# Softmax and key-stage transposes moved to VectorE blocks, values loaded in long runs, in a fused attention and two-layer kernel

## The chip, the cores and the metric

One core of a Trainium2 chip runs the whole program. The metric is the device time of one execution in microseconds (us): the median of the runs, all of them on the chip. The engines have separate in-order queues: TensorE (PE, with its weight loads PEld), VectorE (DVE), ScalarE (ACT), GpSimd (POOL), and SyncE (SP), which in this kernel only issues DMAs.

## The reference

```python
def sm_attn(qq, kk, vv):
    s = scale * np.matmul(qq, kk.transpose(0, 1, 3, 2))
    s = s - np.max(s, axis=-1, keepdims=True)
    a = np.exp(s)
    a = a / (np.sum(a, axis=-1, keepdims=True) + 1e-09)
    return np.matmul(a, vv)
p_packed = sm_attn(p, k, v)          # 32 packed rows attend over 576 keys
out = sm_attn(q, p_packed, p_packed) # 576 queries attend over the 32
...
xn = x / rms * rms_g                 # x: (4608, 512), RMS norm over 512
g = xn @ w_gate
silu = g * (1.0 / (1.0 + np.exp(-g)))
val = xn @ w_val
x = silu * val @ w_out
...
h = x @ w_in
g = h * np.cos(h)
return (g @ w_out).astype(np.float32)
```

Sizes: batch 8, 8 heads, 576 positions, head width 64, 32 packed rows; 4608 tokens of 512; inner widths 1536 and 2048. The arrays q, k, v, p are float32; the weights of the first layer and of the second come as 64-bit floats and are narrowed on the chip.

## The kernel before

The program has four stretches, and a hand-written order (`manual_schedule`) fixes the sequence on every engine in the first three.

**Key stage.** A loop `for i in range(NG + 2)` runs over 16 units (8 batches, two groups of 4 heads). SP loads the packed rows (`load_k`: `pn`, and the keys `kn`, 128 rows with runs of 4608 bytes) four units ahead and the values (`load_v`) two units ahead. The values go in three DMAs of 192 KB, each to 32 partitions in runs of 1536 bytes, into a tile `vn` with 16 rows of padding. For a unit, PE transposes the keys (`u_kt`, tile `kp`, copied by ACT into `kT`), multiplies packed rows with keys (`u_s1`, tile `s1`; for units below `S_PAD` = 11 by a weight tile padded to 128 columns), DVE takes the maximum, ACT the exponential (`u_e`, tile `e`). `u_et` of the unit before transposes the exponentials: six PE transposes into `et`, two ACT copies into `eT`. `u_pp` multiplies them with the values: 6 chunks of 96 positions times 4 heads, each a product of 128 rows by 32 columns by 64; a float32 product is two passes on PE, so 48 passes. `u_fin` transposes the result and stores it to DRAM. Between these, weights of the first layer are narrowed on DVE (`narrow_b`, `wy`, `ny`), and three `unit` calls multiply packed values with weights (`mps`).

**Query attention.** `attend(b)` is a generator. Each `next` on it emits one step. Steps: transposes of queries (`qtp`, copied by ACT to `qT`), scores `sp` (32 packed rows by 288 queries for 4 heads, in two PSUM banks), a copy to `sT` (one half on ACT, one on DVE), PE transposes `stp`, maximum and subtraction on DVE from PSUM into `s` (96 rows), two exponentials on ACT, sums, reciprocals and products on DVE, PE transposes `atp` back with ACT copies into `at`, then products `xp` whose squares give the RMS factor (`a_x`), the root (`a_r`, a POOL power), its spread over rows (`a_b`, transposes `rb`, DVE products) and a split in two parts (`a_p`). `ATT_ORD` and `ATT_ORD0` give the order of the last part, and "-" is an empty step. `attend(0)` runs in the key stage from unit 5 on: one step in iteration 5 and three in each later one, `ATT_U` = 31 in all.

**First layer.** For each batch, 24 iterations: `gv_block` (12 products of 128 by 128 by 288), a silu, a product, a split, and `acc_block` (6 products of 128 by 128 by 512) for the iteration three back. `att_step` spreads the 37 steps of `attend(b + 1)` over the 48 half iterations of batch b, so seven attentions run here, for batches 1 to 7. All of this shares the four PSUM buffers `mm`.

**Second layer.** `h_block` and `o_block`, over 9 chunks of 512 tokens and 16 tiles of 128.

SP's queue issues all DMAs in program order.

Of the kernel before, what the change touches and what calls it, by code (L numbers as in the profile page):

```python
# [20 lines left out]
def kernel(  # L21
# [20 lines left out]
    CP = 96  # L42
# [19 lines left out]
    REST = S - 512  # L62
    V_P = 16
# [154 lines left out]
    def attend(b):  # L218
        s = a1.tile([CP, NC_, H, NP], F32, tag="s", name="s")
        for g in range(2):  # L220
            qTs = []
            for j in (2 * g, 2 * g + 1):
                qv = qn.pop(4 * b + j)
                qT = a2.tile([128, 2, HALF], F32, tag="qT", name="qT")
                for i in range(2):
                    tp = psb[0].tile([128, HALF], F32, tag="mm", name="qtp")
                    for c in range(CH):
                        nc.tensor.transpose(  # L228
                            tp[:, c * CP:(c + 1) * CP], qv[:, i, 2 * c:2 * c + 2, :].rearrange("p c d -> p (c d)"),
                            ident[:CP, :CP],  # L230
                        )
                    nc.scalar.activation(out=qT[:, i], in_=tp, func=AF.Copy)
# [12 lines left out]
            nc.scalar.activation(out=sT[:, 0], in_=sp[0], func=AF.Copy)  # L245
            nc.vector.tensor_copy(sT[:, 1], sp[1])
            yield
            for r in range(2):
                st_p = psb[0].tile([CP, CH, 4, NP], F32, tag="mm", name="stp")
                for c in range(CH):  # L250
                    nc.tensor.transpose(
                        st_p[:, c].rearrange("p h n -> p (h n)"), sT[:, r, c * CP:(c + 1) * CP], ident
                    )
                mx = a2.tile([CP, CH, 4], F32, tag="amx", name="amx")
                nc.vector.tensor_reduce(out=mx, in_=st_p, op=ALU.max, axis=AX.X)
                nc.vector.tensor_tensor(
                    out=s.rearrange("p (c t) h n -> p c t h n", t=2)[:, :, r, 4 * g:4 * g + 4, :], in0=st_p,
                    in1=mx.unsqueeze(3).to_broadcast([CP, CH, 4, NP]), op=ALU.subtract,
                )
            yield  # L260
        n_s = 8 * CH
        hv = [s[:, hf * CH:(hf + 1) * CH].rearrange("p c h n -> p (c h) n") for hf in range(2)]
        for sf in hv:
            nc.scalar.activation(out=sf, in_=sf, func=AF.Exp, scale=scale)
            yield "e"
        for sf in hv:
            sm = a2.tile([CP, 2, n_s], F32, tag="sm", name="sm")
# [4 lines left out]
            if b:  # L272
                yield
            nc.vector.tensor_tensor(
                out=sf, in0=sf, in1=sm[:, 1].unsqueeze(2).to_broadcast([CP, n_s, NP]), op=ALU.mult
            )
            yield

        def transposed(hf, kt):
            tp = psb[0].tile([128, HALF], F32, tag="mm", name="atp")  # L280
            for c in range(CH):
                nc.tensor.transpose(
                    tp[:, c * CP:(c + 1) * CP],
                    s[:, hf * CH + c, 4 * kt:4 * kt + 4, :].rearrange("p h n -> p (h n)"), ident[:CP, :CP],
                )
            return tp

        z = {}

        def a_t(hf, kt):  # L290
            if (hf, kt) == (0, 0):
# [33 lines left out]

        def a_b(hf, _):
            at, ri = z["at"], z["ri"]
            rb = psb[0].tile([128, HALF], F32, tag="mm", name="rb")
            for c in range(CH):
                nc.tensor.transpose(  # L330
                    rb[:, c * CP:(c + 1) * CP], ri[:, 1, 2 * c + hf:2 * c + hf + 1].to_broadcast([CP, 128]),
                    ident[:CP, :CP],
                )
            nc.vector.tensor_tensor(
                out=at[:, :, hf], in0=at[:, :, hf], in1=rb.unsqueeze(1).to_broadcast([128, 2, HALF]), op=ALU.mult
            )

# [10 lines left out]

    v_t = [u2.tile([128, 4, NC_, D], F32, tag=f"vn{x}", name="vn", bufs=1) for x in range(3)]
    for x in range(2):  # L350
        nc.vector.memset(v_t[x], 0.0)
    e_pad = u2.tile([128, 2 * V_P + S], F32, tag="e", name="e", bufs=1)
    for x in (slice(0, V_P), slice(V_P + S, 2 * V_P + S)):
        nc.vector.memset(e_pad[:, x], 0.0)
    nat_k, nat_v = {}, {}
# [39 lines left out]
    def u_kt(i, ms):  # L395

        z = st[i]
        kT, kn = z["kT"], z["kn"]
        kv = kT.rearrange("q h (t m p) -> q h t m p", t=CH, m=CH)
        for m in ms:  # L400
            kp = ps_2.tile([128, CH * 128], F32, tag="kp", name="kp")
            for t in range(CH):
                r = 2 * (CH * m + t)
                nc.tensor.transpose(
                    kp[:, t * 128:(t + 1) * 128], kn[:, r:r + 2, :].rearrange("p c d -> p (c d)"), ident
                )
            nc.scalar.activation(
                out=kv[:, :, :, m, :], in_=kp.rearrange("q (t h p) -> q h t p", t=CH, h=4), func=AF.Copy
            )
# [21 lines left out]
    def u_e(i):  # L431
        z = st[i]
        s1, mx = z["s1"], z["mx"]
        e = e_pad[:, V_P:V_P + S].rearrange("p (a s) -> p a s", a=2)
        nc.scalar.activation(
# [3 lines left out]
    def u_et(i):  # L439
        z = st[i]  # L440
        eT = u2.tile([128, NC_, 128], F32, tag="eT", name="eT", bufs=1)
        for hf in range(2):
            et = ps_2.tile([128, CH, 128], F32, tag="kp", name="et")
            for c in range(CH):
# [7 lines left out]
    def u_pp(i):  # L452
# [179 lines left out]
    u_kt(0, range(CH))  # L632
    nc.gpsimd.memset(v_t[2], 0.0)
    w_q, wo_q = [], []
# [370 lines left out]
    def o_out(n, t):  # L1005
# [8 lines left out]
        while off < 128:  # L1014
            if n < B:
                b, u = n, t * 128 + off
            else:
                b, u = divmod(t * 128 + off, REST)
                u += TOK
            c, pp = divmod(u, CP)  # L1020
            m = min(128 - off, CP - pp)
            dst = out[b * S:(b + 1) * S].rearrange("(p c) d -> c p d", c=NC_)[c, pp:pp + m, :]
# [58 lines left out]
```

## Time and profile before

| quantity | value |
|---|---|
| runs | 1687.13, 1689.0, 1690.26 us; median 1689.0 |
| span of the profiled execution | 1681.2 us |
| between that span and the median | 7.8 us |
| PE busy | 1628.8 us, 97% of the span |
| DVE, ACT, POOL busy | 60%, 50%, 4% |
| key stage | 0 to about 155 us |
| first layer | about 155 to 860 us |
| second layer | about 860 us to the end |

The profile is of one execution. Its span runs from the first to the last instruction; the device time of a run also holds what lies before and after. No device time of the profiled execution itself is listed, so the span stands for it, and the 7.8 us are taken as constant. PE's busy time overstates its work, since matmuls overlap and their ends are modelled: the cost of a group is read from the starts of what comes before and after it.

### The profile page before, as it was taken

The numbers are of one execution on the slowest core, as the hardware profiler recorded it, in microseconds if no ns is written. First come the engines' busy times: TensorE is split into PE (matmuls) and PEld (weight loads), VectorE is DVE, ScalarE is ACT, GpSimd is POOL, SyncE is SP. The second block draws the span as 40 slices with busy tenths as digits, with TensorE's granted clock in tenths as the row PEclk, the third lists the DMA queues.
The fourth block names the chain that finished last, engine by engine and source line by source line (L and its number), as shares of the span: only waits on it lengthen the run. The fifth ranks groups of instructions, "written<-read, shape, count | busy, mean of one in ns | idle before, by whom it ended". The sixth has DMA issues, their size and how long they took to land.

```text
span 1681.2 us, 26128 instructions
## 1 busy us (share of the span) xinstructions
PE 1628.8 (97%) x10112; PEld 1325.8 (79%) x10112; DVE 1008.5 (60%) x1890; ACT 845.2 (50%) x1587; POOL 73.9 (4%) x74
## 2 busy tenths in 40 slices
PE   7877999999999999999999999999999999999998
PEld 5545868788888788888888888888888888888887
DVE  3577985566565666665435665656565656565554
ACT  4455555455454545454434554545454545454443
POOL 1001430000000000000110000000000000000000
PEclk9887999999999999999999999999999999999999
DMA  9996744454535454544363020101010101000001
GB/s 253 285 247 173 226 158 153 145 183 139 195 120 179 143 176 144 170 127 131 104 239 106 25 63 1 51 1 51 0 50 1 50 1 41 11 0 26 1 26 25
DMA packets 103580, 177.35 MB, mean 105 GB/s; under 512 B 39456, under 2 KB 55840, under 8 KB 103456
## 3 DMA queue, kind: packets, MB, share of 16 engines
q1 hardware_dynamic: 103456, 175.68, 34.4%
q8 instruction: 80, 1.31, 0.3%
q14 instruction: 44, 0.36, 0.1%
HBM read 134.22 MB, written 41.42 MB: 104 GB/s over the span
## 4 chain that ended last, share of the span: by engine, by line
PE 89%; DMA 5%; DVE 3%; ACT 1%; issue 1%; SPq 1%; POOL 0%; DVEq 0%; POOLq 0%; ACTq 0%
PE hp L160 8%; PE hp L159 8%; PE hp L158 8%; PE ops L160 8%; PE ops L159 8%; PE ops L158 8%; PE gv L158 6%; PE acc L158 6%; PE gv L159 6%; PE gv L160 6%; PE acc L160 6%; PE acc L159 6%; PE mps L580 3%; DMA kn<-in_k_dram 2%; PE qtp L228 1%
## 5 line engine op out<-in xcount | busy, mean ns | idle before, releaser
L158 PE MATMUL gv<-apt,wmhl 128*128 128x288 f32 x768 | 237.8, 310 | 3.0 <-DVE silu L766 2.0
L159 PE MATMUL gv<-apt,wmhl 128*128 128x288 f32 x768 | 228.6, 298 | 0.2 <-DVE apt L107 0.2
L160 PE MATMUL gv<-apt,wmhl 128*128 128x288 f32 x768 | 228.0, 297 | 0.0
L159 PE MATMUL hp<-xhl,wmhl 128*128 128x512 f32 x576 | 224.1, 389 | 0.0
L160 PE MATMUL hp<-xhl,wmhl 128*128 128x512 f32 x576 | 224.1, 389 | 0.0
L158 PE MATMUL ops<-w2hl,ghl 128*128 128x512 f32 x576 | 224.1, 389 | 0.0
L159 PE MATMUL ops<-w2hl,ghl 128*128 128x512 f32 x576 | 224.1, 389 | 0.0
L158 PE MATMUL hp<-xhl,wmhl 128*128 128x512 f32 x576 | 223.9, 389 | 0.0
L160 PE MATMUL ops<-w2hl,ghl 128*128 128x512 f32 x576 | 222.3, 389 | 0.0
L981 ACT ACTIVATE r<-r 128x512 f32<-128x512 f32 x144 | 91.1, 633 | 250.0 <-DVE r L980 250.0
L989 DVE TENSOR_TENSOR r<-r,hp 128x512 f32<-128x512 f32 x144 | 98.9, 687 | 164.8 <-ACT r L982 164.8
L158 PEld LDWEIGHTS gv<-apt,wmhl 128*128 128x128 f32 x768 | 146.0, 190 | 44.3 <-issue 17.6
L158 PE MATMUL acc<-shl,wohl 128*128 128x512 f32 x432 | 176.6, 409 | 0.2 <-DMA shl<-s 0.2
L160 PE MATMUL acc<-shl,wohl 128*128 128x512 f32 x432 | 170.7, 395 | 2.4 <-POOL wohl L546 2.4
L159 PE MATMUL acc<-shl,wohl 128*128 128x512 f32 x432 | 169.6, 393 | 0.0
L773 ACT ACTIVATE shl<-silu 128x288 fp32r<-128x288 f32 x192 | 85.4, 445 | 159.6 <-DVE silu L766 158.4
L766 DVE TENSOR_TENSOR silu<-silu,gv 128x288 f32<-128x288 f32 x192 | 86.5, 451 | 125.5 <-PE gv L160 106.2
L976 ACT ACTIVATE kk<-hp,magic 128x512 f32<-128x512 f32 x144 | 99.1, 688 | 117.3 <-PE hp L160 117.1
L159 PEld LDWEIGHTS gv<-apt,wmhl 128*128 128x128 f32 x768 | 146.2, 190 | 4.4 <-DVE apt L107 0.5
L160 PEld LDWEIGHTS gv<-apt,wmhl 128*128 128x128 f32 x768 | 145.8, 190 | 0.0
L977 DVE TENSOR_SCALAR kk<-kk 128x512 f32<-128x512 f32 x144 | 61.4, 426 | 116.1 <-ACT kk L976 116.0
L158 PEld LDWEIGHTS ops<-w2hl,ghl 128*128 128x128 f32 x576 | 108.2, 188 | 22.6
(127 smaller groups left out, 2708.4 us busy)
## 6 DMA issues: line engine op xcount, KB each, us to landing
wy<-wy SPq DMA_DIRECT2D x96, 512.0 KB, 4.5
kn<-in_k_dram SPq DMA_DIRECT2D x16, 576.0 KB, 7.4
vn<-in_v_dram SPq DMA_DIRECT2D x48, 192.0 KB, 6.5
qnat<-in_q_dram SPq DMA_DIRECT2D x32, 288.0 KB, 4.1
x_dram<-x SPq DMA_DIRECT2D x18, 512.0 KB, 3.0
x1raw<-x_dram SPq DMA_DIRECT2D x18, 512.0 KB, 4.0
raw<-in_moe_w_in_dram SPq DMA_DIRECT2D x16, 512.0 KB, 4.2
raw<-in_moe_w_out_dram SPq DMA_DIRECT2D x16, 512.0 KB, 4.2
```

What stands on the lines that cost most here:

```text
L158: nc.tensor.matmul(ps, lhi, rhi, start=first, stop=False)
L159: nc.tensor.matmul(ps, lhi, rlo, start=False, stop=False)
L160: nc.tensor.matmul(ps, llo, rhi, start=False, stop=last)
L228: nc.tensor.transpose(tp[:, c * CP:(c + 1) * CP], qv[:, i, 2 * c:2 * c + 2, :].rearrange("p c d -> p (c d)"), ident[:CP, :CP],)
L580: nc.tensor.matmul(ps[kt][h * NP:(h + 1) * NP], ppT[b // 4][rows, 4 * kt + h, n:n + NP], w_y[2 * u + kt][rows, j], start=True, stop=True,)
L766: nc.vector.tensor_tensor(out=t, in0=t, in1=pss[1], op=ALU.mult)
L773: nc.scalar.activation(out=sh[:, 0, cols], in_=t, func=AF.Copy)
L976: nc.scalar.activation(out=kk, in_=hp, func=AF.Identity, scale=1.0 / TWO_PI, bias=magic[:, 0:1])
L977: nc.vector.tensor_scalar(out=kk, in0=kk, scalar1=-MAGIC, scalar2=None, op0=ALU.add)
L981: nc.scalar.activation(out=r, in_=r, func=AF.Abs)
L989: nc.vector.tensor_tensor(out=r, in0=r, in1=hp, op=ALU.mult)
```

## The change

- Scores `sp` are transposed by DVE, in blocks of 32 by 32, straight from PSUM into a tile `st` of 128 rows; `sT`, `stp` and their copies go. Maximum and subtraction run on 128 rows by 576, and so do sums and products. The exponential is one ACT instruction over 128 rows by 1152.
- The weights go back by one DVE block transpose per group of heads (`a_t`), without PE and ACT.
- In the key stage one DVE block transpose of 128 by 576 replaces six PE transposes and two ACT copies (`u_et`). The values are loaded by one DMA per unit, 128 rows with runs of 4608 bytes, and three memsets go. `u_pp` runs 18 chunks of 32 positions times 4 heads, each product 32 rows by 32 columns by 64: 144 passes in place of 48.
- The two query transposes of a pair of heads are one step, and so are the two halves of `a_b`. `attend` has 27 steps in place of 37, and 23 (`ATT_U`) in place of 31 in the key stage.
- The order of tokens in the columns changes, and the output's row index with it.

```diff
-    ATT_U, U_ATT = 31, 5
+    ATT_U, U_ATT = 23, 5
-    ATT_ORD = "t00 t10 - x00 t01 t11 - x10 - - r00 - - b00 b10 p00 p10"
-    ATT_ORD0 = "t00 t10 x00 x01 t01 t11 x10 x11 - r00 - b00 b10 p00 p10"
+    ATT_ORD = "t00 - x00 t10 - x10 - - r00 - - b00 p00 p10"
+    ATT_ORD0 = "t00 x00 x01 t10 x10 x11 - r00 - b00 p00 p10"
-    ATT_FROM, ATT_TO, ATT_FROM0, ATT_TO0, N_ATT = 0, 48, 10, 45, 37
+    ATT_FROM, ATT_TO, ATT_FROM0, ATT_TO0, N_ATT = 0, 48, 10, 45, 27
...
+                tps = [psb[0].tile([128, HALF], F32, tag="mm", name="qtp") for _ in range(2)]
...
-                    if i == 0:
-                        yield
...
-            sT = a1.tile([128, 2, HALF], F32, tag="sT", name="sT")
-            nc.scalar.activation(out=sT[:, 0], in_=sp[0], func=AF.Copy)
-            nc.vector.tensor_copy(sT[:, 1], sp[1])
+            st = a2.tile([128, 2, NB, NP], F32, tag="st", name="st", bufs=1)
+            for r in range(2):
+                nc.vector.transpose(st[:, r].rearrange("p c n -> p (c n)"), sp[r])
             yield
-            for r in range(2):
-                st_p = psb[0].tile([CP, CH, 4, NP], F32, tag="mm", name="stp")
-                for c in range(CH):
-                    nc.tensor.transpose(
-                        st_p[:, c].rearrange("p h n -> p (h n)"), sT[:, r, c * CP:(c + 1) * CP], ident
-                    )
-                mx = a2.tile([CP, CH, 4], F32, tag="amx", name="amx")
...
+            nc.vector.tensor_reduce(out=mx, in_=sv, op=ALU.max, axis=AX.X)
...
+        nc.scalar.activation(out=s, in_=s, func=AF.Exp, scale=scale)
+        yield "e"
...
-            nc.scalar.activation(out=z["at"][:, kt, hf], in_=transposed(hf, kt), func=AF.Copy)
+            nc.vector.transpose(
+                z["at"][:, kt].rearrange("p r x -> p (r x)"), s[:, kt].rearrange("p r c n -> p (r c n)")
+            )
...
-        vn = nat_v[i] = v_t[i % len(v_t)]
-        vs = v[b, 4 * g:4 * g + 4].rearrange("h (p m c) d -> m p h c d", m=CH, c=NC_)
-        for m in (0, 2, 1):
-            nc.sync.dma_start(out=vn[V_P + m * 32:V_P + (m + 1) * 32], in_=vs[m])
+        vn = nat_v[i] = u5.tile([128, CH * NC_, D], F32, tag="vn", name="vn", bufs=3)
+        nc.sync.dma_start(out=vn, in_=v[b, 4 * g:4 * g + 4].rearrange("h (p c) d -> (h p) c d", c=CH * NC_))
...
-        for hf in range(2):
-            et = ps_2.tile([128, CH, 128], F32, tag="kp", name="et")
-            for c in range(CH):
-                cc = hf * CH + c
-                nc.tensor.transpose(et[:, c, :], e_pad[:, cc * CP:cc * CP + 128], ident)
-            nc.scalar.activation(out=eT[:, hf * CH:(hf + 1) * CH], in_=et, func=AF.Copy)
+        nc.vector.transpose(eT.rearrange("p a c n -> p (a c n)"), z["e"].rearrange("p a s -> p (a s)"))
...
-        for c in range(NC_):
+        n_c = CH * NC_
+        for c in range(n_c):
             for h in range(4):
                 r = slice(h * NP, (h + 1) * NP)
                 nc.tensor.matmul(
-                    pp[r], eT[:, c, r], vn[:, h, c % CH * 2 + c // CH, :], start=c == 0, stop=c == NC_ - 1
+                    pp[r], eT[r, c % 2, c // 2], vn[r, c], start=c == 0, stop=c == n_c - 1
                 )
```

## Rows read from the trace of the kernel before

**Rows 1.** Busy time by stretch; in brackets the instructions, then TensorE clock, DMA share, GB/s.

```profile
0.00:50.00 50.00, 39.30 (x451) 29.12 (x451) 19.50 (x53) 22.35 (x53) 5.07 (x23) 0.93 1.01 260
50.00:100.00 50.00, 39.62 (x511) 26.12 (x517) 31.97 (x77) 24.57 (x62) 1.46 (x5) 0.90 1.04 281
100.00:150.00 50.00, 33.72 (x480) 20.83 (x484) 34.51 (x83) 26.68 (x66) 1.92 (x3) 0.76 0.76 213
150.00:200.00 50.00, 45.56 (x356) 38.02 (x349) 44.85 (x87) 28.04 (x61) 18.52 (x11) 0.93 0.78 227
...
350.00:400.00 50.00, 50.00 (x374) 40.77 (x373) 30.24 (x63) 27.34 (x56) 0.00 (x0) 1.00 0.50 159
```

**Rows 2.** The chain of waits in order of time: start, us, what.

```profile
10.47 7.18 DMA kn<-in_k_dram
17.72 8.71 DMA kn<-in_k_dram
...
109.80 0.87 DVE sm L268
...
128.98 3.10 DMA q<-tf
...
224.71 1.29 POOL wohl L546
```

**Rows 3.** Timeline of PE in the first layer: start, us, engine, line, operation.

```profile
392.64 0.41 PE L282 MATMUL atp<-ident,s 96*128 96x96 f32 x3
392.83 0.38 PE L158 MATMUL gv<-apt,wmhl 128*128 128x288 f32 x1
...
445.14 0.82 PE L251 MATMUL stp<-ident,sT 128*96 128x128 f32 x6
445.71 0.38 PE L158 MATMUL gv<-apt,wmhl 128*128 128x288 f32 x1
445.93 0.30 PE L159 MATMUL gv<-apt,wmhl 128*128 128x288 f32 x1
446.06 0.29 PE L160 MATMUL gv<-apt,wmhl 128*128 128x288 f32 x1
...
455.97 1.09 PE L580 MATMUL mps<-wy,ppT 64*32 64x512 f32 x16
456.99 0.40 PE L158 MATMUL gv<-apt,wmhl 128*128 128x288 f32 x1
```

**Rows 4.** Groups of instructions, 0 to 262 us: busy us, mean ns, idle before.

```profile
L427 DVE TENSOR_REDUCE mx<-s 128x1 f32<-128x576 f32 x16 | 11.9, 746 | 17.5 <-PE s L419 17.5
...
L256 DVE TENSOR_TENSOR s<-stp,amx 96x384 f32<-96x384 f32 x8 | 4.4, 554 | 0.3
...
L274 DVE TENSOR_TENSOR s<-s,sm 96x768 f32<-96x768 f32 x4 | 3.8, 948 | 0.0
...
L246 DVE COPY sT<-sp 128x288 f32<-128x288 f32 x4 | 1.8, 451 | 1.0 <-PE sp L241 1.0
```

**Rows 5.** Timeline of PE in the key stage, exponentials' transposes and value products.

```profile
26.47 0.87 PE L446 MATMUL et<-ident,e 128*128 128x128 f32 x6
27.28 2.21 PE L419 MATMUL s<-kT,pT 64*128 64x288 f32 x16
...
40.17 1.51 PE L460 MATMUL pp<-vn,eT 128*32 128x64 f32 x48 [1.82 <-DVE pT L392]
41.61 1.54 PE L446 MATMUL et<-ident,e 128*128 128x128 f32 x6
...
54.11 0.88 PE L460 MATMUL pp<-vn,eT 128*32 128x64 f32 x48
54.92 1.04 PE L580 MATMUL mps<-wy,ppT 64*32 64x512 f32 x2
```

**Rows 6.** DMA issues, 0 to 160 us: count, KB each, median us from issue to landing.

```profile
kn<-in_k_dram SPq DMA_DIRECT2D x16, 576.0 KB, 7.4
vn<-in_v_dram SPq DMA_DIRECT2D x48, 192.0 KB, 6.5
```

More of the change, by code (lines that the diff above doesn't have):

```diff
@@ L218, in attend @@
     def attend(b):
-        s = a1.tile([CP, NC_, H, NP], F32, tag="s", name="s")
+        NB = HALF // NP
+        s = a1.tile([128, 2, 2, NB, NP], F32, tag="s", name="s")
         for g in range(2):
@@ L224, in attend @@
                 qT = a2.tile([128, 2, HALF], F32, tag="qT", name="qT")
+                tps = [psb[0].tile([128, HALF], F32, tag="mm", name="qtp") for _ in range(2)]
                 for i in range(2):
-                    tp = psb[0].tile([128, HALF], F32, tag="mm", name="qtp")
                     for c in range(CH):
                         nc.tensor.transpose(
-                            tp[:, c * CP:(c + 1) * CP], qv[:, i, 2 * c:2 * c + 2, :].rearrange("p c d -> p (c d)"),
-                            ident[:CP, :CP],
-                        )
-                    nc.scalar.activation(out=qT[:, i], in_=tp, func=AF.Copy)
+                            tps[i][:, c * CP:(c + 1) * CP],
+                            qv[:, i, 2 * c:2 * c + 2, :].rearrange("p c d -> p (c d)"), ident[:CP, :CP],
+                        )
+                for i in range(2):
+                    nc.scalar.activation(out=qT[:, i], in_=tps[i], func=AF.Copy)
                     qTs.append(qT[:, i])
-                    if i == 0:
-                        yield
                 load_q()
@@ L243, in attend @@
                     )
-            sT = a1.tile([128, 2, HALF], F32, tag="sT", name="sT")
-            nc.scalar.activation(out=sT[:, 0], in_=sp[0], func=AF.Copy)
-            nc.vector.tensor_copy(sT[:, 1], sp[1])
+            st = a2.tile([128, 2, NB, NP], F32, tag="st", name="st", bufs=1)
+            for r in range(2):
+                nc.vector.transpose(st[:, r].rearrange("p c n -> p (c n)"), sp[r])
             yield
-            for r in range(2):
-                st_p = psb[0].tile([CP, CH, 4, NP], F32, tag="mm", name="stp")
-                for c in range(CH):
-                    nc.tensor.transpose(
-                        st_p[:, c].rearrange("p h n -> p (h n)"), sT[:, r, c * CP:(c + 1) * CP], ident
-                    )
-                mx = a2.tile([CP, CH, 4], F32, tag="amx", name="amx")
[L255 to L259, printed above, removed]
-            yield
[L261 to L267, printed above, removed]
+            sv = st.rearrange("p r c n -> p (r c) n")
+            mx = a2.tile([128, 2 * NB], F32, tag="amx", name="amx")
+            nc.vector.tensor_reduce(out=mx, in_=sv, op=ALU.max, axis=AX.X)
+            nc.vector.tensor_tensor(
+                out=s[:, g].rearrange("p r c n -> p (r c) n"), in0=sv,
+                in1=mx.unsqueeze(2).to_broadcast([128, 2 * NB, NP]), op=ALU.subtract,
+            )
+            yield
+        nc.scalar.activation(out=s, in_=s, func=AF.Exp, scale=scale)
+        yield "e"
+        for g in range(2):
+            sf = s[:, g].rearrange("p r c n -> p (r c) n")
+            sm = a2.tile([128, 2, 2 * NB], F32, tag="sm", name="sm")
             nc.vector.tensor_reduce(out=sm[:, 0], in_=sf, op=ALU.add, axis=AX.X)
@@ L271, in attend, with a_t @@
             yield
-            if b:
-                yield
             nc.vector.tensor_tensor(
-                out=sf, in0=sf, in1=sm[:, 1].unsqueeze(2).to_broadcast([CP, n_s, NP]), op=ALU.mult
+                out=sf, in0=sf, in1=sm[:, 1].unsqueeze(2).to_broadcast([128, 2 * NB, NP]), op=ALU.mult
             )
             yield
-        def transposed(hf, kt):
-            tp = psb[0].tile([128, HALF], F32, tag="mm", name="atp")
-            for c in range(CH):
[L282 to L286, printed above, removed]
         z = {}
-        def a_t(hf, kt):
-            if (hf, kt) == (0, 0):
+        def a_t(kt, _):
+            if kt == 0:
                 z["at"] = a1.tile([128, 2, 2, HALF], F32, tag="at", name="at")
-            nc.scalar.activation(out=z["at"][:, kt, hf], in_=transposed(hf, kt), func=AF.Copy)
+            nc.vector.transpose(
+                z["at"][:, kt].rearrange("p r x -> p (r x)"), s[:, kt].rearrange("p r c n -> p (r c n)")
+            )
         def a_x(kt, part):
@@ L324, in a_r, with a_b @@
             nc.gpsimd.tensor_tensor(out=ri[:, 1], in0=ri[:, 0], in1=mhalf, op=ALU.pow)
-        def a_b(hf, _):
+        def a_b(*_):
             at, ri = z["at"], z["ri"]
[L328 to L332, printed above, removed]
-                )
-            nc.vector.tensor_tensor(
-                out=at[:, :, hf], in0=at[:, :, hf], in1=rb.unsqueeze(1).to_broadcast([128, 2, HALF]), op=ALU.mult
-            )
+            rb = [psb[0].tile([128, HALF], F32, tag="mm", name="rb") for _ in range(2)]
+            for hf in range(2):
+                for c in range(CH):
+                    nc.tensor.transpose(
+                        rb[hf][:, c * CP:(c + 1) * CP],
+                        ri[:, 1, 2 * c + hf:2 * c + hf + 1].to_broadcast([CP, 128]), ident[:CP, :CP],
+                    )
+            for hf in range(2):
+                nc.vector.tensor_tensor(
+                    out=at[:, :, hf], in0=at[:, :, hf], in1=rb[hf].unsqueeze(1).to_broadcast([128, 2, HALF]),
+                    op=ALU.mult,
+                )
         def a_p(hf, _):
@@ L347, in attend @@
             yield nxt[:1]
[L349 to L354, printed above, removed]
     nat_k, nat_v = {}, {}
@@ L398, in u_kt @@
         kT, kn = z["kT"], z["kn"]
[L399 removed]
+        kv = kT.rearrange("q h (c p) -> q h c p", p=NP)
         for m in ms:
@@ L407, in u_kt @@
             nc.scalar.activation(
-                out=kv[:, :, :, m, :], in_=kp.rearrange("q (t h p) -> q h t p", t=CH, h=4), func=AF.Copy
+                out=kv[:, :, CH * m:CH * (m + 1), :], in_=kp.rearrange("q (t h p) -> q h t p", t=CH, h=4), func=AF.Copy
             )
@@ L440, in u_et @@
         z = st[i]
-        eT = u2.tile([128, NC_, 128], F32, tag="eT", name="eT", bufs=1)
-        for hf in range(2):
-            et = ps_2.tile([128, CH, 128], F32, tag="kp", name="et")
-            for c in range(CH):
-                cc = hf * CH + c
-                nc.tensor.transpose(et[:, c, :], e_pad[:, cc * CP:cc * CP + 128], ident)
-            nc.scalar.activation(out=eT[:, hf * CH:(hf + 1) * CH], in_=et, func=AF.Copy)
+        eT = u2.tile([128, 2, HALF // NP, NP], F32, tag="eT", name="eT", bufs=1)
+        nc.vector.transpose(eT.rearrange("p a c n -> p (a c n)"), z["e"].rearrange("p a s -> p (a s)"))
         z["eT"], mx = eT, z["mx"]
@@ L1020, in o_out @@
             c, pp = divmod(u, CP)
+            c = 2 * (c % CH) + c // CH
             m = min(128 - off, CP - pp)
```

4 lines of the change are left out of this document (1 added, 3 removed).

## Prediction

> **What bounds the kernel now.** I read the busy time by stretch first. From 350 to 400 us PE is busy all 50 us at a granted clock of 1.00 (the level of 2.4 GHz), while DVE is busy 30.24 and ACT 27.34 [rows 1]. That stretch stands for the whole first layer after its first batch: PE's own instructions set the time there. From 0 to 100 us the DMA share is 1.01 and 1.04, at 260 and 281 GB/s, with PE busy 39 of 50 and DVE 19.50 and 31.97; from 100 to 150 no engine is full (PE 33.72, DVE 34.51, DMA 0.76, clock 0.76) [rows 1]. So the key stage has two parts, a first one paced by transfers and a second one paced by chains from engine to engine.
>
> The chain of waits, read second, says the same in order of time. Up to 50 us it runs from one load of keys to the next: the one issued at 10.47 lands after 7.18 us, and the next is issued at 17.72 and takes 8.71 [rows 2]. The second goes out as soon as the first has landed. Between them lie seven other issues of SP, so it is as if eight DMAs may be under way at once, and their number counts as well as their bytes. After 100 us the chain holds DVE work of the softmax (109.80) and a store awaited behind SP's issues (128.98, 3.10 us) [rows 2]. Third, PE's timeline gives the prices of single groups, from where the next one starts [rows 3, 5].
>
> **The first layer, per attention.** Removed from PE: two groups of six transposes `stp`. One starts at 445.14 and the next product at 445.71, 0.57 us; that product's successor comes 0.22 us later (445.93) where 0.13 is usual (445.93 to 446.06), so the group costs 0.57 + 0.09 = 0.66 us [rows 3]. Two of them: 1.32. Also removed: four groups of three transposes `atp`, each 0.19 us (392.64 to 392.83) plus the same 0.09: 4 x 0.28 = 1.12 [rows 3]. The query transposes stay, but eight groups of three become four of six, which saves four changes of 0.09: 0.36. Two groups of `rb` become one: 0.09. Sum: 1.32 + 1.12 + 0.36 + 0.09 = 2.89 us.
>
> Six attentions (batches 2 to 7) run where PE is full: 6 x 2.89 = 17.3 us. The seventh runs in the first batch, where DVE is busy 44.85 of 50 us from 150 to 200 and the chain goes through POOL's split of the output weights (224.71, 1.29 us) [rows 1, 2]. There I count half, 1.4 us, with bounds of 0 and 2.9. Together 18.7 us, between 17 and 20 if nothing new stalls.
>
> What hides the work added to DVE: its idle 20 us in 50 [rows 1]. The trace shows no block transpose. Nearest are DVE's 128x288 copy from PSUM, 451 ns, and its pass over 128x576, 746 ns [rows 4]; I take these two, since all these rows cost about one column per nanosecond and some 150 ns beside it. Bounds: 0.4 us for 128x576, as if it ran at twice the rate, and 1.5, half of it. Per attention DVE loses two copies (0.9), four subtractions over 96x384 at 0.554 and four reductions of the same elements (4.4), two products over 96x768 at 0.948 and two sums alike (3.8): 9.1 us. It gains four transposes of 128x288 (1.8), two of 128x576 (1.5) and two each of maximum, subtraction, sum and product over 128x576 (8 x 0.746 = 6.0): 9.3 us. So DVE stays where it was, and ACT loses six copies and part of the exponentials. If a transpose cost double, DVE would have 3.3 us more per batch of some 88 us (155 to 860 us over eight) and still be idle for a third. Without that cover PE would wait for `sp`'s two buffers, which now come free after two DVE transposes in a row in place of a copy on each of two engines, 0.45 us later. The next products that want them stand behind six accumulations, 1.4 us at the gate products' rate (0.13 us for 288 columns, so 0.23 for 512), so I cost it at nothing.
>
> **The key stage.** Per unit PE loses six `et` transposes, 26.47 to 27.28, 0.81 us. The products go from 48 to 144 passes. The 48 take 54.11 to 54.92, 0.81 us or 17 ns each, and 40.17 to 41.61, 1.44 us or 30 ns each, at the slower pace that PE shows there [rows 5]. Before, four column tiles work side by side; afterwards four diagonal tiles do, on the same 64 columns, so I take the same pace: 144 x 17 = 2.43 us, with 144 x 30 = 4.3 as the upper bound and no reason for a gain per pass. PE gets 2.43 - 0.81 - 0.81 = +0.8 us per unit, 13 us over 16 units; at 30 ns, with `et` at some 1.5 (the row at 41.61), 4.3 - 1.44 - 1.5 = +1.4, or 22. PE has some 37 us of idle time from 0 to 150 us [rows 1], which hides most. I count it where PE sets the pace, about four units: 4 x 1.0 = +4 (0 to +15).
>
> The Trainium skill ("TensorE: Matmul & The Clock Gate", section "Wait — 56ns, not 53.3ns?") puts the least distance between the starts of two matmuls at about 25 ns. The 48 passes here go at 17 ns, so the trace does not bear it out; by it the products would take 144 x 25 = 3.6 us per unit.
>
> DVE gets a transpose of 128x576 per unit, 0.75 us (0.4 to 1.5). It hides where transfers set the pace. Where DVE's queue is on the chain, about four units, it delays the next maximum, and with it the exponential and the next products: +3 (+1 to +8). The path from the exponential to `eT` itself becomes shorter, one instruction in place of transposes and copies.
>
> Values: 48 loads of 192 KB become 16 of 576 KB, the shape of the key loads, which land in 7.4 us as one where three value loads stand at 6.5 each [rows 6]. The 9.4 MB of values take 36 us of transfer at 260 GB/s. At the 281 GB/s of the second stretch they would take 33.5 [rows 1]. The gain has no row of its own: the lower end is 0, the upper takes the 36 us to a third less, 12 us, if three short runs cost half as much again as one long one. I take 5, as only part of the stage waits for transfers. Two issues fewer per unit also let loads and stores pass earlier under the limit of eight, with the 3.10 us at 128.98 as the nearest row [rows 2]: 3 us (0 to 5).
>
> Attention: 23 steps at three per iteration end in iteration 13; 31 end in 15. The softmax sums that stand on the chain at 109.80 [rows 2] move into iterations paced by transfers, and the last two iterations carry none of it. One sum there is 0.87 us on the chain, and there are two sums and two products with them: 3 us (0 to 6). The three memsets at the start, and the one DMA that now writes 128 rows, are off the path.
>
> Sum of the key stage: +4 + 3 - 5 - 3 - 3 = -4 us, with bounds of about -17 and +14.
>
> **Total.** 18.7 + 4 = 22.7 us off 1681.2 gives a span of 1658.5; with the 7.8 us around it 1666.3 us, against a median of 1689.0.
>
> **The rivals.**
>
> *The key stage gains nothing or grows.* The products take 30 ns a pass and the DVE transposes stand on the chain: +5 to +14. For it: the clock is already at 0.76 from 100 to 150 us [rows 1]. Against: PE's idle time. Time: 1689.0 - 18.7 + 8 = 1678.
>
> *The key stage gains much.* Transfers gain 10 and the stores and the attention 8, with +4 against: -14. Time: 1656.
>
> *The row tiles block each other (the other side).* All products of a unit write one PSUM bank, now from four row tiles. If these take turns, a pass costs four times 17 ns, 68 ns, and a unit 144 x 68 = 9.8 us, +8.2 net, 131 us over 16 units. Less PE's 37 us idle this is some +94 in the key stage, and the time is 1689.0 - 18.7 + 94 = 1764. It decides from the point where the stage grows by 18.7 us: with the 37 us hidden, 56 us or 3.5 us per unit, (3.5 + 1.62) / 144 = 36 ns a pass. Against it: the weight products `mps` write each of two banks from two row tiles. Sixteen passes of 512 columns take 455.97 to 456.99, 1.02 us, or 64 ns each [rows 3]. A pass of 512 columns alone would take 0.23 us even at the rate of the gate products (0.13 us for 288 columns), which have the faster number format. So at least 3.6 passes run side by side there, and they do not take turns as a whole. The Trainium skill ("TensorEngine Tiling (Array Packing)", section "Gotcha 1: PSUM Pressure") says that different row tiles cannot access the same bank simultaneously, which speaks against this change; the row on `mps` does not show such a stall.
>
> *PE's saving is not returned.* Something else in the first layer (softmax on DVE, the four buffers) takes it: then only the key stage counts, 1689 - 4 = 1685. Against: PE waits for nothing in 350 to 400 us [rows 1].
>
> **How the numbers follow.** Chances: forecast (key stage -9 to +5) 0.55; key stage grows 0.19; key stage gains much 0.15; saving not returned 0.06; row tiles block 0.05. The likeliest gives 1666, its own range 1661 to 1676. The range reaches into the two neighbours on either side, to 1653 and 1682. About 0.2% (3.4 us) is what a measurement can tell from no change. Faster: the first three and half of the fourth, 0.92; same 0.03; slower 0.05.
>
> **What would show it.** Right: in the first layer, no `stp` and `atp`, and the distance from one `sp` group to the one a batch later shorter by 2.9 us, with PE still full. In the key stage, 144 passes in about 2.4 us, transposes near 0.75 and 0.45 us on DVE, a value load landing like a key load, and the first gate product some 4 us before 155. Wrong: passes over 36 ns apart, DVE transposes near 1.5 us with DVE full in the first batch, or idle time of PE before gate products.

## The result and the profile after

The changed kernel takes 1700.39 us (median; 1698.54 to 1702.72), beside 1688.07 us for the kernel before on the same chip: a ratio of 1.0073 [1.0059, 1.0087]. It is slower by some 12 us, where 1666 was forecast.

Where the time went is read from two instants on PE's timeline: the first gate product `gv`, which ends the key stage, and the first product `hp`, which begins the second layer. Between them lies the first layer.

| profiled execution | before | after |
|---|---|---|
| first gate product | 154.74 us | 185.24 us |
| first layer | 738.3 | 727.4 |
| from first `hp` to the end | 788.2 | 788.3 |
| span | 1681.2 | 1700.9 |

The last stretch is the same to 0.2 us in all the runs below, and each run's device time is 1.7 to 2.2 us above its span. Each kernel was profiled once. Its first layer lies between 725.9 and 728.2 us in the seven kernels with the attention of the kernel after, while the runs of one kernel spread over 2 to 11 us; so I put that spread down to the key stage. Below, "key stage" is the median time less 1.9, the first layer of the profile and 788.2 (or .3), and a difference of 2 us in it says nothing. It is 159.7 us before and 182.8 after: +23.1, where -4 was forecast. (The one execution profiled before was some 5 us quicker than that kernel's median. The 7.8 us between its span and the median was therefore mostly chance.) The first layer gives back 10.9 us, where 18.7 was forecast.

Busy time by stretch of the kernel after, columns as in [rows 1]:

```profile
0.00:50.00 50.00, 35.76 (x727) 27.15 (x727) 18.31 (x48) 15.10 (x35) 4.28 (x22) 0.97 0.83 263
50.00:100.00 50.00, 35.42 (x761) 27.97 (x762) 27.81 (x66) 17.33 (x41) 1.76 (x4) 0.86 0.71 215
100.00:150.00 50.00, 35.74 (x741) 24.86 (x740) 29.42 (x71) 16.85 (x41) 1.99 (x4) 0.73 0.51 158
150.00:200.00 50.00, 33.95 (x732) 27.23 (x733) 34.35 (x76) 18.94 (x42) 4.17 (x4) 0.83 0.61 180
350.00:400.00 50.00, 50.00 (x380) 40.91 (x379) 29.19 (x61) 22.77 (x52) 1.83 (x1) 1.00 0.53 171
```

The DMA share, 1.01 and 1.04 in the first two stretches of [rows 1], is down to 0.83 and 0.71. Transfers no longer pace the key stage, yet no engine is full there: PE is busy 35 of 50 us, DVE 18 to 34. That is the mark of a chain from engine to engine. The chain of waits shows the chain (start, us, what):

```profile
98.21 3.01 issue
...
104.06 3.01 PE pp L434 x113
...
114.03 0.69 DVE wy L152
114.72 0.69 DVE eT L420
...
115.64 0.67 DVE mx L405
...
116.41 0.29 DVE pT L370
...
116.74 3.91 PE pp L434 x144
...
167.13 4.29 issue
171.41 3.87 PE pp L434 x144
```

From 114 to 121 us the same turn can be followed on the timeline of all engines (start, us, engine, line, operation, then the idle time before it and who ended it):

```profile
114.03 0.69 DVE L152 SCALAR_TENSOR_TENSOR wy<-wo,wy 128x512 int32<-128x512 int32 x1
114.64 0.77 DVE L420 STREAM_TRANSPOSE eT<-e 128x576 f32<-128x576 f32 x1
...
115.56 0.74 DVE L405 TENSOR_REDUCE mx<-s 128x1 f32<-128x576 f32 x1
...
116.41 0.28 DVE L370 COPY pT<-pt 128x128 f32<-128x128 f32 x1
...
116.74 3.75 PEld L434 LDWEIGHTS pp<-vn,eT 32*32 32x32 f32 x144 [5.21 <-DVE pT L370]
```

DVE works off its queue in order: the narrowing of weights, then the transpose of the exponentials, the maximum, and the copy `pT`. That copy frees the PSUM buffer which PE wants next (`pt`, `kp`, `pp`, `tp` share the tag `kp`). The products come only after it, and DVE's scaling `cd` and what stands behind it wait for the products, 47.7 us of DVE's time in the stage: a loop between two in-order queues, one turn for each of 16 units. Waits of DVE and PE in the key stage, 0 to 185.24 us (who waited, for whom: us, times, longest; "issue" means that the profile shows nothing that was awaited):

```profile
DVE cd L438 <- PE pp L434: 47.7, 16, 5.7
...
PE pp L434 <- issue: 18.6, 8, 4.3
PE kp L382 <- DVE pT L370: 12.2, 7, 4.2
...
PE s L397 <- issue: 6.4, 3, 3.0
...
PE pp L434 <- DVE pT L370: 5.0, 1, 5.0
```

What was forecast of single prices came true. DVE's transposes take 770, 768 and 462 ns (forecast 746, 746, 451), and a load of values lands in 5.0 us (first the groups of DVE, then the DMA issues, both as in [rows 4, 6]):

```profile
L420 DVE STREAM_TRANSPOSE eT<-e 128x576 f32<-128x576 f32 x16 | 12.3, 770 | 1.8 <-ACT e L413 1.8
...
L245 DVE STREAM_TRANSPOSE st<-sp 128x288 f32<-128x288 f32 x4 | 1.7, 462 | 2.5 <-PE sp L240 2.5
...
L274 DVE STREAM_TRANSPOSE at<-s 128x576 f32<-128x576 f32 x2 | 1.5, 768 | 0.0
```

```profile
vn<-in_v_dram SPq DMA_DIRECT2D x16, 576.0 KB, 5.0
```

PE's timeline shows the 144 passes in one unbroken burst, and in one that is broken:

```profile
26.66 1.80 PE L434 MATMUL pp<-vn,eT 32*32 32x64 f32 x113
31.28 0.81 PE L434 MATMUL pp<-vn,eT 32*32 32x64 f32 x31 [2.81 <-issue]
...
37.43 2.21 PE L434 MATMUL pp<-vn,eT 32*32 32x64 f32 x144
39.57 1.73 PE L397 MATMUL s<-kT,pT 64*128 64x288 f32 x12
```

The whole burst takes 37.43 to 39.57, 2.14 us or 14.9 ns a pass, at a granted clock of 1.00, the level of 2.4 GHz. That is no more than the 17 ns of the column tiles before, so the row tiles do not block each other. The Trainium skill ("TensorEngine Tiling (Array Packing)", section "Gotcha 1: PSUM Pressure") says that different row tiles cannot access one PSUM bank at the same time; this burst does not bear that out. Nor does it bear out the least distance of some 25 ns between the starts of two matmuls that the Trainium skill gives ("TensorE: Matmul & The Clock Gate", section "Wait — 56ns, not 53.3ns?"). The burst at 116.74, after 5 us of waiting, took 3.91 us, 27 ns a pass, at a granted clock of 0.54, close to the level of 1.2 GHz. A wait in the loop can thus be paid twice: once itself, once in the slower passes behind it.

### The profile page after: what moved, and what is told of

It is laid out like the page before. It is cut to its first block, busy times and chain, and to the rows that moved or that the text cites. A ratio compares the mean times of both kernels' runs of the same rounds, so it can differ in the third digit from the quotient of the medians.

```text
span 1700.9 us, 28440 instructions
## 1 busy us (share of the span) xinstructions
PE 1629.9 (96%) x11360; PEld 1330.5 (78%) x11360; DVE 1013.9 (60%) x1902; ACT 794.3 (47%) x1487; POOL 74.0 (4%) x73
## 4 chain that ended last, share of the span: by engine, by line
PE 90%; DVE 4%; issue 3%; ACT 1%; DMA 1%; POOL 1%; SPq 0%; ACTq 0%; POOLq 0%; DVEq 0%
PE hp L159 8%; PE hp L157 8%; PE hp L158 8%; PE ops L159 8%; PE ops L157 8%; PE ops L158 8%; PE gv L157 6%; PE acc L157 6%; PE acc L159 6%; PE acc L158 5%; PE gv L158 5%; PE gv L159 5%; PE pp L434 3%; PE mps L554 3%; PE xp L285 1%
```

## The experiments

Twelve kernels ran. "Key stage" and "first layer" are as defined above; the ratio is to the kernel before on the same chip, whose median was 1684.2 to 1687.6 us there.

| kernel | median us | ratio [interval] | key stage | first layer |
|---|---|---|---|---|
| before | 1688.07 | 1 | 159.7 | 738.3 |
| after | 1700.39 | 1.0073 [1.0059, 1.0087] | 182.8 | 727.4 |
| 1 attention alone | 1665.51 | 0.9875 [0.9854, 0.9897] | 147.2 | 728.2 |
| 2 key stage alone | 1714.13 | 1.0161 [1.0141, 1.0181] | 184.8 | 739.2 |
| 3 a third of the products | 1667.30 | 0.9878 [0.9862, 0.9894] | 151.2 | 725.9 |
| 4 wide products | 1690.93 | 1.0022 [1.0009, 1.0035] | 172.9 | 727.8 |
| 5 `pT` on ACT | 1698.86 | 1.0054 [1.0031, 1.0077] | 181.2 | 727.5 |
| 6 small `eT` | 1693.26 | 1.0034 [1.0019, 1.0050] | 177.1 | 726.0 |
| 7 values in long runs | 1674.90 | 0.9923 [0.9910, 0.9936] | 146.5 | 738.2 |
| 8 attention, x10 later | 1659.72 | 0.9834 [0.9814, 0.9855] | 149.0 | 720.6 |
| 9 one load of values | 1658.67 | 0.9843 [0.9818, 0.9869] | 147.9 | 720.6 |
| 10 attention late | 1667.43 | 0.9885 [0.9865, 0.9905] | 154.3 | 723.0 |
| 11 narrowing late | 1680.70 | 0.9968 [0.9956, 0.9979] | 163.4 | 727.1 |
| 12 the same on 8 | 1671.03 | 0.9906 [0.9891, 0.9922] | 158.8 | 722.1 |

**1 and 2: one part of the change each.** The first has `attend` of the kernel after with the key stage of the kernel before, the second the reverse.

In 1, against the kernel before:

```diff
-    ATT_U, U_ATT = 31, 5
+    ATT_U, U_ATT = 23, 5
+                nc.vector.transpose(st[:, r].rearrange("p c n -> p (c n)"), sp[r])
...
```

In 2, against the kernel after:

```diff
-    ATT_U, U_ATT = 23, 5
+    ATT_U, U_ATT = 31, 5
-                nc.vector.transpose(st[:, r].rearrange("p c n -> p (c n)"), sp[r])
...
```

> The attention's part of the change with the key stage of before. Theory A (the key stage's products are what costs; the first layer gains): the key stage ends near 155 us as before, the first layer is 10 to 11 us shorter, as it is from the first gate product on in the changed kernel (1700.9 - 185.2 = 1515.7 us there, 1681.2 - 154.7 = 1526.5 before): 1674 to 1679 us. Rival B (the attention's block transposes on VectorE delay the key stage): the key stage ends at 165 us or later and the time is 1685 or more.

> The key stage's part alone, with the attention of before. Theory A: the key stage is some 25 to 30 us longer and nothing is given back: 1708 to 1718 us. Rival B: the attention makes half or more of the loss, so the key stage ends before 172 us and the time is 1703 or less.

The attention's part gains more than either theory had, 12.5 us in the key stage besides 10.1 in the first layer. The key stage's part loses 25.1. With it, the attention's part is worth only 2.0 us there (184.8 to 182.8). So all of the loss comes from the key stage's part, and 1665.51 us beats both kernels.

**3 and 4: what of the products costs?** The third runs 48 of the 144 passes; the fourth runs 48 passes of 192 columns each, as many columns as after with a third of the instructions.

In 3 and then in 4, against the kernel after:

```diff
-        n_c = CH * NC_
+        n_c = NC_
```

```diff
-                    pp[r], eT[r, c % 2, c // 2], vn[r, c], start=c == 0, stop=c == n_c - 1
+                    pp3[r], eT[r, c % 2, c // 2], vn[r, 3 * c:3 * c + 3].rearrange("p c d -> p (c d)"),
+                    start=c == 0, stop=c == n_c - 1,
```

> The changed kernel with 6 of the 18 chunks of the value products, 48 passes per unit in place of 144; two thirds of the sum over the keys are left out. Theory A1 (the number of PE instructions: the engine waits for its instructions to be fetched) and theory A2 (the PE time of the products, in a loop with VectorE) both expect the key stage to end 20 us or more earlier, near 160, and 1670 to 1680 us. Rival C (the block transpose on VectorE before each maximum, and the lower clock): less than 10 us back, 1690 or more.

> The changed kernel with 48 passes per unit of 192 columns in place of 144 of 64: the same columns go through the array in a third of the instructions; the products are not those of the reference (each weight meets three chunks of values). Theory A1 (instructions): the waits for issue go, the key stage ends near 165 and the time is 1675 to 1684 us, close to the run with a third of the products. Theory A2 (PE time of the products): the burst still takes 2 us or more and the time stays at 1692 to 1701.

The groups of `pp` on PE (busy us, mean ns) in the kernel after, in 3 and in 4:

```profile
L434 PE MATMUL pp<-vn,eT 32*32 32x64 f32 x2304 | 49.5, 257 | 23.7 <-issue 18.6 <-DVE pT L370 5.0
```

```profile
L434 PE MATMUL pp<-vn,eT 32*32 32x64 f32 x768 | 18.9, 261 | 18.9 <-issue 18.2 <-DVE pT L370 0.7
```

```profile
L435 PE MATMUL pp<-vn,eT 32*32 32x192 f32 x768 | 48.9, 417 | 19.2 <-issue 14.3 <-DVE pT L370 4.9
```

Both results miss their ranges: 3 is faster than either theory had, and 4 falls between them. In 3 the group loses 30.6 us of busy time and the key stage 31.6. In 4 the busy time stays and the stage still loses 9.9 us. From 4 to 3, with the same number of passes, 30.0 us of busy time are worth 21.7 of the stage's length: most of the products' time counts, where the forecast had most of it hidden. PE works through 192 columns in 43 ns (48 passes in 2.08 us) and through 64 in 14.9, so columns set the price of a pass, and 9.9 us go with the number of instructions. In the kernel after, PE stops for 1.2 to 3.0 us in the midst of five bursts of `pp` or `s`, for which the profile shows nothing that is missing: at 28.46, 48.18, 98.21, 134.00 and 154.43 us, 11.3 us in all. In each of the first three there is one transfer of the instruction queue (q8), and ahead of each of the last two one that ends as the stop begins (133.0 to 134.1, 153.4 to 154.4 us). In the first window:

```profile
q8 instruction: 1, 0.02, 2.2%
```

The key stage has 22 such transfers of 16 KB after and 10 in 4, which has no such stop. The other kernels with 144 passes (2, 5, 6, 11) stop in the same way, 11.6 to 15.4 us in all, counting stops over 0.8 us; among those with 48 passes only 9 does, once, for 1.05 us. All these 29 stops end 1.2 to 1.6 us after the end of such a transfer; in the kernel after the transfers end at 30.1, 49.7, 99.9, 134.1 and 154.4 us, and PE goes on at 31.28, 51.03, 101.22, 135.41 and 155.64. So I read these stops as PE waiting for instructions, though the supply of instructions was not changed by itself.

**5: which wait?** ACT copies `pT` in place of DVE.

```diff
-        nc.vector.tensor_copy(pT[:, :, :NP], pt.rearrange("p (h n) -> p h n", h=4))
+        nc.scalar.activation(out=pT[:, :, :NP], in_=pt.rearrange("p (h n) -> p h n", h=4), func=AF.Copy)
```

> The changed kernel, but ACT and not DVE copies the transposed packed rows (pT) out of PSUM, so that the next key transposes of PE no longer wait for DVE's queue. Theory (loop through the in-order queues of PE and DVE): PE waits 17 us for DVE's pT copy in the key stage; most of that goes, the first gate product comes 6 to 15 us before 185, and the time is 1685 to 1695 us. Rival (the products' time on PE alone sets the stage): no wait of that size is saved, the first gate product stays within 3 us of 185, and the time is 1697 to 1703. Second rival (the wait only moves to DVE's transpose of the exponentials): 1697 to 1703 too, with PE's holes ahead of pp grown by as much.

By the medians the stage stays within 1.6 us; two of the five runs, at 1690.9 and 1694.1 us, were quicker than the others (1698.9 to 1701.5). The 17 us of waits for `pT` are gone, but what the profile books as issue ahead of `pp` has grown from 18.6 to 30.2. Without the stops inside bursts (5.4 and 9.4 us) it has grown from 13.2 to 20.8 (waits of PE, then the timeline of 5):

```profile
PE pp L434 <- issue: 30.2, 11, 4.2
```

```profile
105.72 0.42 DVE L142 TENSOR_SCALAR ny<-ny 128x512 f32<-128x512 f32 x1
...
109.61 0.69 DVE L152 SCALAR_TENSOR_TENSOR wy<-wo,wy 128x512 int32<-128x512 int32 x1
110.22 0.77 DVE L420 STREAM_TRANSPOSE eT<-e 128x576 f32<-128x576 f32 x1
...
111.09 4.06 PE L434 MATMUL pp<-vn,eT 32*32 32x64 f32 x144 [4.17 <-issue]
```

The profile calls this wait "issue". The products start 0.10 us after DVE's transpose has ended (110.22 + 0.77 = 110.99), and so it is at the other long ones. The transpose itself stands behind eight narrowing passes, 105.72 to 110.22. So the second rival holds in the main: much of the wait only moved one place on in DVE's queue, 7.6 us of it by these figures, and not as much again as had gone.

**6: the transpose's own time.**

```diff
-        nc.vector.transpose(eT.rearrange("p a c n -> p (a c n)"), z["e"].rearrange("p a s -> p (a s)"))
+        eT = eT0
+        nc.vector.transpose(
+            eT.rearrange("p a c n -> p (a c n)")[:, :64], z["e"].rearrange("p a s -> p (a s)")[:, :64]
+        )
```

> The changed kernel, but DVE transposes only 64 of the 576 columns of the exponentials in each unit, and the others stay zero (most of the exponentials are left out). This takes some 0.65 us of DVE from each of 16 units, 10.4 us. Theory (each turn of the loop carries the transpose in full): the first gate product comes 7 to 13 us before 185, and the time is 1687 to 1694 us. Rival (DVE's idle time covers it, as forecast for 12 of 16 units): at most 4 us sooner, 1696 to 1702.

The transpose now takes 236 ns, 0.53 us less in each of 16 units, 8.5 us in all. The time is within the theory's range; the key stage is 5.7 us shorter, and by the profiles 8.4 (first gate product at 176.84). DVE's idle time covers little of it.

**7 and 9: is it the number of loads or the length of the runs?** 7 is the kernel before with the values' load of the change; 9 is kernel 8 (below) with one load of 96 rows per unit, in the old runs.

In 7, against the kernel before:

```diff
-        for m in (0, 2, 1):
-            nc.sync.dma_start(out=vn[V_P + m * 32:V_P + (m + 1) * 32], in_=vs[m])
+        nc.sync.dma_start(
+            out=vn.rearrange("p h c d -> p (h c) d")[:, :CH * NC_],
+            in_=v[b, 4 * g:4 * g + 4].rearrange("h (p c) d -> (h p) c d", c=CH * NC_),
+        )
```

In 9, against 8, in the same place and in `u_kt`:

```diff
+            out=vn[V_P:V_P + CP].rearrange("x h c d -> x h (c d)"),
+            in_=v[b, 4 * g:4 * g + 4].rearrange("h (x c) d -> x h (c d)", c=NC_),
...
-        kv = kT.rearrange("q h (t m p) -> q h t m p", t=CH, m=CH)
+        kv = kT.rearrange("q h (t p m) -> q h t m p", t=CH, m=CH)
```

> The kernel before, but each unit's values are loaded by one DMA of 128 rows in runs of 4608 bytes in place of three (the products get the values in another order than the reference wants; the work is the same). This is the transfers' part of the change alone. Theory (transfers pace the first part of the key stage before): the first gate product comes 3 to 10 us before 154.7, and the time is 1677 to 1684 us. Rival (the key stage does not wait for values): within 2 us, 1685 to 1690.

> The kernel of the eighth experiment (the attention's change with x10 later, 1659.7 us) with the values in one DMA per unit: 96 rows in order of position, runs of 1536 bytes as before, 576 KB; the copies of the key transposes write the columns of the scores in that order. The seventh experiment (long runs on 128 rows, one DMA per unit) gained 12.7 us. Theory A (the number of DMAs under way counts): it gains about as much here, 8 to 13 us, time 1647 to 1652 us. Theory B (the length of the runs counts): 0 to 3 us, 1656 to 1661. Half each: 1652 to 1656.

The values' new load alone takes 13.2 us off the key stage, more than forecast for all that concerns transfers (8), and the time is below the theory's range. One load in short runs gains nothing that can be measured over 8. The stretch from 50 to 100 us and the landing of values, in 7:

```profile
50.00:100.00 50.00, 37.11 (x500) 24.36 (x500) 31.80 (x76) 26.05 (x63) 2.39 (x6) 0.90 0.88 287
```

```profile
vn<-in_v_dram SPq DMA_DIRECT2D x16, 576.0 KB, 5.6
```

and in 9, with ACT's copies of the key transposes (groups: busy us, mean ns):

```profile
50.00:100.00 50.00, 36.34 (x477) 23.75 (x473) 35.29 (x85) 26.49 (x60) 1.73 (x5) 0.86 1.05 280
```

```profile
vn<-in_v_dram SPq DMA_DIRECT2D x16, 576.0 KB, 8.2
```

```profile
L395 ACT ACTIVATE kT<-kp 128x384 f32<-128x384 f32 x48 | 30.6, 688 | 36.3 <-PE kp L392 36.3
```

At nearly the same GB/s the DMA engines are busy 0.88 of the time in 7 and 1.05 in 9, so it is not the number of loads. Two things are left that 7 changes and 9 does not: the runs are three times as long, and they go to 128 rows of the tile in place of 96. The length of the runs is the likelier cause, but no run separates the two. One reservation more: in 9 the copies `kT` write with a stride and take 688 ns in place of some 490, 9.5 us more of ACT, which may hide a small gain.

**8 and 10: the attention's part.** In the kernel after, a batch of the first layer is 1.89 us shorter than before, not 2.89. The groups of `xp` show why (PE's timeline after):

```profile
381.18 0.72 PE L240 MATMUL sp<-qT,bq 64*32 64x288 f32 x16
...
430.33 0.71 PE L285 MATMUL xp<-at,cl 32*64 32x288 f32 x6
431.31 0.72 PE L285 MATMUL xp<-at,cl 32*64 32x288 f32 x10 [0.27 <-DVE silu L739]
...
467.24 0.71 PE L240 MATMUL sp<-qT,bq 64*32 64x288 f32 x16
```

From `sp` to `sp` a batch later takes 467.24 - 381.18 = 86.06 us, 87.95 before. The second group of `xp` breaks off, since it wants PSUM buffers of `mm` that come free behind a DVE product; from start to start it takes about 1 us more. Kernel 8 puts it one step later, on the kernel of experiment 1; kernel 10 adds empty steps to the first attention of 8.

In 8, against 1:

```diff
-    ATT_ORD = "t00 - x00 t10 - x10 - - r00 - - b00 p00 p10"
+    ATT_ORD = "t00 - x00 t10 - - x10 - r00 - - b00 p00 p10"
```

In 10, against 8:

```diff
-    ATT_U, U_ATT = 23, 5
+    ATT_U, U_ATT = 31, 5
-    ATT_ORD0 = "t00 x00 x01 t10 x10 x11 - r00 - b00 p00 p10"
+    ATT_ORD0 = "- - - - - - - - t00 x00 x01 t10 x10 x11 - r00 - b00 p00 p10"
```

> The kernel of the first experiment (the attention's change alone, 1665.5 us), with the second group of RMS products (x10) one step later in the order of steps. Theory (the products xp of x10 wait for the four buffers, which come free only after a silu on DVE, some 1 us per batch): the xp wait goes, a batch takes 85.0 to 85.4 us in place of 86.0, and the time is 1658 to 1662 us. Rival (the buffers are short at any step, and the wait moves to another tile): a batch stays at 85.8 to 86.2, 1664 to 1667 us.

> The kernel of the eighth experiment, with eight empty steps ahead of the last part of the first attention, so that its 31 steps end in the same iteration of the key stage as before the change (15 in place of 13). Theory (the key stage of the attention's change is shorter because the attention ends earlier, as forecast): 3 to 10 us are lost, time 1663 to 1670 us. Rival (it is shorter because the transposes of the scores and their copies are gone from PE and ACT): within 2 us, 1658 to 1662.

Kernel 8 on PE's timeline:

```profile
346.83 0.71 PE L241 MATMUL sp<-qT,bq 64*32 64x288 f32 x16
...
398.95 0.74 PE L286 MATMUL xp<-at,cl 32*64 32x288 f32 x16
...
431.90 0.71 PE L241 MATMUL sp<-qT,bq 64*32 64x288 f32 x16
```

`xp` runs whole, and a batch takes 431.90 - 346.83 = 85.07 us: 2.88 less than before. The first layer loses 17.7 us in all. 10 gives back 7.7 us, 5.3 of them in the key stage. (The two ran on different chips; the intervals of their ratios do not overlap.) Thus about half of the 10.7 us that the attention saves there in 8 is the earlier end of its last part, as the theory has it. The empty steps stand behind the softmax, whose steps stay early in 10, so what their move is worth was not tested. The other 2.4 us lie in the first layer, about as much as kernels with the same attention differ there.

**11 and 12: the order of DVE's queue.** In 11 the second half of the narrowing goes behind the next unit's transpose, maximum and `pT` copy, all else as after. 12 is the same edit on 8.

```diff
-        if i < NG:
-            w_late()
-            w_late = lambda: None
```

> The changed kernel, but the second half of each weight's narrowing (two DVE passes of 0.7 us for each of one to three weights per unit) stands in DVE's queue behind the transpose of the exponentials, the maximum and the pT copy of the next unit, and not ahead of them. Nothing is left out. Theory (PE's holes in the key stage are waits for DVE's queue, in which the transpose of the exponentials stands behind the narrowing): PE's waits ahead of kp and pp (17 and some 12 us) fall by half or more, the first gate product comes 6 to 16 us before 185, and the time is 1684 to 1695 us. Rival (the wait moves to the next work on DVE, the scaling cd and the weights that are narrowed late): within 3 us, 1697 to 1703.

> The same edit on the kernel of the eighth experiment (the attention's change with x10 later, key stage of before, 1659.7 us). Theory (maximum and pT copy behind the narrowing cost time here too, though the exponentials are transposed on PE): 2 to 8 us sooner, 1652 to 1658 us. Rival (transfers set the pace of this key stage, and DVE's order doesn't count): within 2 us, 1658 to 1662.

PE's waits in the key stage of 11:

```profile
PE s L397 <- issue: 10.6, 3, 5.6
PE kp L382 <- DVE pT L370: 6.8, 10, 1.9
PE pp L434 <- issue: 5.7, 4, 2.3
```

No work is taken away, and the key stage is 19.4 us shorter. The waits ahead of `kp` and `pp` fall from 35.8 us (18.6 + 12.2 + 5.0) to 12.5, and the products themselves from 49.5 to 39.8 us of busy time, with a mean granted clock of 0.91 in place of 0.84 in the stage. The gain is larger than expected. The stops inside bursts remain, 13.9 us in all, most of them in `s`. In 12 the same edit costs 9.8 us in the key stage, which neither expectation had. There PE transposes the exponentials and does not wait for DVE in each turn, and what the narrowing releases comes later. PE waits in 12:

```profile
PE mps L567 <- DVE wy L153: 6.5, 3, 4.1
```

In 8 only PE's weight loads show this wait, 3.1 us of it against 9.2 in 12. That it makes up most of the 9.8 us was not tested. The order is right or wrong only with respect to the loop that sets the pace.

## Why the prediction was wrong

**The step that failed** is the cover in the key stage: "which hides most. I count it where PE sets the pace, about four units: 4 x 1.0 = +4", of PE's 37 us of idle time. With it goes the term for DVE, "Where DVE's queue is on the chain, about four units, it delays the next maximum", at +3. Measured one at a time, the added passes are worth 31.6 us (experiment 3; 9.9 of it goes with the number of instructions, 4, for which the forecast has no term), the transpose on DVE 5.7 x 576 / 512 = 6.4 (6), the values' load -13.2 (7). The sum is +24.8, where experiment 2 shows +25.1 and the attention's part takes off 2.0 in this stage. That the sum fits so well is partly luck: 7 was measured in the key stage of before and the others in that of after, and the six `et` transposes taken from PE have no run of their own. What compares with the forecast of +7 is experiment 2 without the transfers' gain, 25.1 + 13.2 = 38 us, if that gain is as large beside the new products as in 7, which no run shows. PE's idle time was not free: it was PE's part of waiting in a loop with DVE, and work added inside a loop lengthens each of its 16 turns. Experiment 11 shows that the price is one of order as much as of work: with all added work in place, 19.4 of the 23.1 us go away. The stated bounds of -17 and +14 are also narrower than the terms' own bounds added up, -22 and +23.

**Prices of single operations** held: DVE's transposes within 4%, passes at 14.9 ns where the clock is full (17 forecast), no turns taken by row tiles, faster loads. The upper bound of 30 ns for a pass was nearly reached too (27 ns), in the burst that follows a wait of 5 us.

**Transfers and issues** (-5, -3): mis-sized, -13.2, a little beyond the upper end of 12 for the transfers alone. The -5 rested on the longer runs, and 7 and 9 agree with that as far as they go. The -3 rested on fewer DMAs under a limit of eight at once, and 9, with two fewer per unit, shows no such gain.

**Attention ends earlier** (-3): half of the mechanism, the later iterations without attention, is shown (10), with 5.3 us; the move of the softmax sums was not tested. In experiment 1 the key stage gained 12.5; what the rest of that comes from stays open. Behind the new loop only 2.0 of it were seen.

**First layer** (-18.7): the 2.89 us removed per attention were right (2.88 in 8), but "if nothing new stalls" was not: the second `xp` group stalled about 1 us per batch on the four `mm` buffers, and 10.9 came back. I looked at `sp`'s buffers for such a stall and not at those of `xp`.

**The rivals.** The key stage that "grows" was the right one, and of its two reasons "the DVE transposes stand on the chain" held, but its +5 to +14 stop short of the 23.1 measured. Row tiles that block did not happen (14.9 ns a pass). That PE's saving is not returned came true in part: 7.8 of the 18.7 us were not.

Kernel 8 is the version to keep of these: attention's part, key stage of before, one step moved; 1.7% faster than before [0.9814, 0.9855]. Kernel 9 is not distinguishable from it.

## What to carry to other kernels

Idle time of an engine covers new work only if the engine waits there for something outside the loop that the work enters. Ask of each added instruction whether its result is awaited, in the same turn, by an engine whose result it awaits in its turn; if so, count it in every turn. When a change frees the resource that paced a stage, work out the next pace before using the old one's slack, and look at what stands ahead of the new instruction in its in-order queue: moving that work behind it was worth more here than the instruction itself.

## What the runs showed of the hardware

PE stopped for 1.2 to 3.0 us within bursts of `pp` or `s` five times in the key stage after, 11.3 us in all; with a third of the passes (3, 4) no burst has such a stop. Each time it went on 1.2 to 1.3 us after a 16 KB transfer of the instruction queue had ended. The DMA engines were busy 0.88 of a stretch at 287 GB/s with values in runs of 4608 bytes to 128 rows (7) and 1.05 at 280 GB/s with runs of 1536 to 96 rows (9). Four diagonal tiles of 32x32 that write one PSUM bank took 14.9 ns a pass at a granted clock of 1.00. A wait that the profile puts down to "issue" can be one for another engine: 4.17 us ahead of `pp` ended 0.10 us after DVE's transpose.
